# Two f tiles of the first side: down products as a 2x2 block product of 256-wide matmuls in place of 512-wide ones, its weights kept for the second side

## The chip, the cores and the metric

One core of a Trainium2 chip runs the whole program. The metric is the device time of one launch in microseconds (us). All figures below come from the page, the times and the trace of the kernel before.

## The reference, cut to what matters

The block is adaLN, a linear attention, a second adaLN and a gated bilinear MLP, all in float32, on one sequence of 2048 tokens with D = 512 and F = 1376. Only its last part is touched:

```
h = _layernorm(x) * (1 + cb) + sb          # x: 2048 x 512, after the attention
g = h @ w_gate                             # 512 x 1376
u = h @ w_up                               # 512 x 1376
x = x + gb * ((g * u) @ w_down)            # 1376 x 512
```

`gb` is a row of 512 factors; the kernel multiplies it into the rows of `w_down`.

## The kernel before

Every float32 operand of a matmul is split into a high part, rounded to the type that TensorE takes (`split`, L206 and L207: ScalarE writes the high part, VectorE or GpSimd the low part as a difference), and a product is three matmuls: high by high, high by low, low by high.

**The MLP.** The tokens are four chunks of 512; a side is two chunks: the first side is chunks 0 and 1, the second chunks 2 and 3. The hidden columns are 11 f tiles of 128 (the last, f 10, has 96). For each side and f tile one call of `block` makes gate and up for both chunks at once, as a 2x2 block product with 7 products instead of 8. Its left factors (`a11`, `s1`, `s2`, `a12`, `s3`, `a22`, `s4`) are pieces, sums and differences of the layer-normed tokens, its right factors the like of the weights. One product is 6 matmuls of 128x512 (L1057), so a block is 42, in the order a11, s1, s2, a12, s3, a22, s4. They go to four PSUM banks, which no other product uses.

Blocks are numbered 0 to 21 here, in their order on TensorE (`order` in the code). The first side's are 0 to 10 with f = 2, 3, 4, 5, 6, 7, 8, 9, 0, 1, 10; the second side's 11 to 21 with f = 0 to 10. Blocks 8 and 9 are thus f 0 and 1, and block 10 is f 10, of the first side; 11 and 12 are f 0 and 1 of the second.

**Down products.** The results of a block, `phi`, are the left operand of the down product, in which f is summed over. There are two ways:

- `down` (L1146 to L1148): for a group of f tiles, a chunk and some of its four quarters of 128 tokens, 3 matmuls of 128x512 for each f tile and quarter into a PSUM bank (`acc`, one of four), then a VectorE add into `x` (L1153) and, when it is the last, a DMA that writes the output. The first side's groups are f 2-3, 4-5, 6-7, 8-9 and 0-1-10. A group's four pieces (`fillers`) are spread over the blocks of the next group, in their point `pe`, between the fifth and the sixth product.
- `Pair` and `pair_steps` (L1223, L1250): two f tiles and two chunks form a 2x2 block product again, 7 steps for each two quarters; a step is 6 matmuls of 128x256, then VectorE adds of 128x256 into `x`. All pairs of f tiles of the second side go this way. `weight_sums` scales the two tiles of `w_down` (VectorE, L1277) and makes sums of them (GpSimd, L1204); `weight_splits` splits them (ScalarE L1214, GpSimd L1215). Steps stand in `queue`, from which each block takes up to 7, at its `POINTS`.

**What sets the order.** There is no scheduler: each engine runs its instructions in the order in which the code records them. A block has named points (`a11`, `s1`, `s2`, `a12`, `s3`, `pe`, `mid`, `s4`) to which jobs are hung (`at`). Nearly all DMAs are issued by SyncE (SP), in order, each after the instruction that it waits for and after the landing of the DMA eight places before it. Tiles come from one pool of 99 buffers, so that a DMA or an instruction may also wait for an older reader of its buffer.

**Transfers around the change.** The left factors of the second side are made during blocks 3 to 9 and written to DRAM (`aside`, L969); `fetch` (L983) brings back 28 tiles of 256 KB for block 11. Right factors are kept in DRAM too (L1034) and come back as 7 tiles for each block from 13 on (L1044); those of blocks 11 and 12 are still in their buffers. `load_down` (L111) loads a tile of `w_down`.

Of the kernel before, what the change touches and what calls it, by code (L numbers as in the profile page):

```python
# [11 lines left out]
ALU = mybir.AluOpType  # L12
# [10 lines left out]
def tile_adaln_block(  # L23
# [12 lines left out]
    nc = tc.nc  # L36
# [11 lines left out]
    NF = len(fts)  # L48
# [16 lines left out]
    def f32(ap):  # L65
        return ap.bitcast(F32)
# [339 lines left out]
    sums = {}  # L406
# [239 lines left out]
    for i in range(4, NT):  # L646
        ch, j = divmod(i, NJ)
        more = ch + 1 < NCH
# [129 lines left out]
    fs, tt = [], []  # L778
# [55 lines left out]
    pairs = [(cut(norm[2].t[k], 3 * P, 4 * P), wq[k]) for k in range(KD)]  # L834
# [230 lines left out]
    todo = []  # L1065
# [94 lines left out]
    class Pair:  # L1160
# [50 lines left out]
        def weight_splits(self, *ms):  # L1211
            for m in ms:
                h, l = B("w", dt=F32R), B("w", dt=F32R)
                nc.scalar.activation(h, self.raw[m], AF.Copy)  # L1214
                nc.gpsimd.tensor_tensor(l, self.raw[m], f32(h), op=ALU.subtract)  # L1215
# [56 lines left out]
    def load_down(f):  # L1272
        f0, n = fts[f]
        return load(w_down[f0:f0 + n, :], "raw")
# [4 lines left out]
    sides = [(0, 1), (2, 3)]  # L1279
# [102 lines left out]
    def split_down(s, f, low=None):  # L1382
        split_d[s, f] = split_raw(raw_d.pop((s, f)), low=low)
# [47 lines left out]
    pair_of = {f: g for g, fs in enumerate(groups) for f in fs[:2]}  # L1431
    weights = {}

    for n, (s, g, f) in enumerate(order):
        groups = groups_of[s]
        first, final = f == groups[g][0], f == groups[g][-1]
        if first:
            if before is not None and before[0] == 0:
                down_jobs(*before)
            for x in groups[g] if s == 0 else ():  # L1440
                raw_d[s, x] = load_down(x)
# [27 lines left out]
        if s == 0:  # L1469
# [3 lines left out]
        if n and order[n - 1][0] == 0:  # L1473
            at["s2"].insert(0, lambda s=order[n - 1][0], f=order[n - 1][2]: split_down(s, f))
# [9 lines left out]
        if s == 1 and f in pair_of:  # L1484
            at_first = f == groups[g][0]
            if at_first:
                pairs[g] = Pair()
                at["pe"].append(lambda xs=groups[g]: raw_d.update({(1, x): load_down(x) for x in xs}))
                sums = lambda g=g, x=groups[g]: pairs[g].weight_sums(raw_d[1, x[0]], raw_d[1, x[1]])
                if g:  # L1490
                    at["mid"].insert(0, sums)
            else:
                if not g:
                    at["s2"].append(sums)
                at["s3"] += [lambda g=g: pairs[g].weight_splits(0, 2)]
                at["mid"] += [lambda g=g: pairs[g].weight_splits(1, 3)]

            def done(i, t, p=pairs[g], at_first=at_first):
                p.f[(("a11", "a21") if at_first else ("a12", "a22"))[i]] = t
                if i == 0:  # L1500
                    todo.append(p.first if at_first else p.second)
        if s == 1:
            if n > NF + 1 and f in pair_of and first:
                queue += [x for js in ((0, 1), (2, 3)) for x in pair_steps(1, pairs[g - 1], js)]
            if f == tail:
                queue += pair_steps(1, pairs[g], (0, 1))
            if first and g:
                at["s2"].append(lambda p=pairs[g - 1]: (p.lows("s1", "s2"), p.second("s4")))
                at.setdefault("a12", []).append(lambda p=pairs[g - 1]: p.lows("a12", "s4", "a22"))
            elif f == tail:  # L1510
                at["s2"].append(lambda p=pairs[g]: (p.lows("s1", "s2"), p.second("s4")))
            for p in POINTS[4:] if n == NF + 2 else POINTS:
                at.setdefault(p, []).append(lambda: queue and queue.pop(0)())
            if f == tail:
                at["a12"].append(lambda p=pairs[g]: p.lows("a12", "s4", "a22"))
                at["s3"].append(lambda: split_down(1, tail))
# [27 lines left out]
    more = pair_steps(1, pairs[len(groups_of[1]) - 1], (2, 3), of=bank, also=with_tail)  # L1544
# [38 lines left out]
```

## Time and profile before

| what | us |
|---|---|
| median of 3 runs (554.57 to 554.84) | 554.71 |
| the profiled execution | 554.69 |
| its span, first to last instruction | 552.5 |
| TensorE busy in it, 2739 matmuls | 546.7 |
| VectorE / ScalarE / GpSimd busy | 421.0 / 297.4 / 177.4 |
| L1057, 924 matmuls of the blocks, busy union | 220.2 |
| L1146 to L1148, 276 matmuls of `down`, busy union | 107.6 |
| L1223, 420 matmuls of the pairs, busy union | 91.8 |

The span is the reading of the trace; 2.2 us of the execution lie around it. Matmuls are pipelined and their ends are modelled, so the duration of one (390 ns at 128x512, 282 ns at 128x256) is longer than the time from its start to the next one's start, which is what it costs. Block times are read from one first matmul to the next: on TensorE blocks 8, 9, 10, 11, 12, 13 and 14 start at 330.62, 345.58, 357.82, 370.29, 388.08, 405.86 and 417.56 us, and block 15 at 432.20.

### The profile page before, as it was taken

How to read it: one execution, taken by the hardware profiler on the slowest of the kernel's cores; microseconds unless marked ns; L12 is line 12 of the kernel's file. 1: busy time of each engine (PE TensorE's matmuls, PEld its weight loads, DVE VectorE, ACT ScalarE, POOL GpSimd, SP SyncE). 2: the span in 40 equal slices, each digit the busy share in tenths (PEclk: the TensorE clock that was granted, in tenths of full speed). 3: DMA queues.
4: the chain of work that ended last, by engine and by line, in shares of the span. 5: the costliest groups of instructions: out<-in, count | busy, mean ns of one | idle time of the engine just before them, and what ended most of it. 6: DMA issues, size and time to landing. Idle time of an engine off the chain costs nothing.

```text
span 552.5 us, 8033 instructions
## 1 busy us (share of the span) xinstructions
PE 546.7 (99%) x2739; PEld 459.7 (83%) x2739; DVE 421.0 (76%) x764; ACT 297.4 (54%) x532; POOL 177.4 (32%) x183
## 2 busy tenths in 40 slices
PE   8999999999999999999999999999999999999997
PEld 6888888888888888888888888878888888888886
DVE  6978779978998998865656767854567877879696
ACT  4875858456467876654545355432442534453540
POOL 2000000003537645353556644400512524242400
PEclk9999999999999999999999999999999999999999
DMA  8910224203230045195888635499585534342004
GB/s 258 374 55 1 76 77 152 77 0 78 78 114 2 0 161 182 39 319 177 285 286 273 223 123 206 152 377 324 176 261 200 180 124 141 129 144 87 0 1 152
DMA packets 58800, 83.75 MB, mean 152 GB/s; under 512 B 6596, under 2 KB 23752, under 8 KB 58760
## 3 DMA queue, kind: packets, MB, share of 16 engines
q1 hardware_dynamic: 56832, 81.68, 43.6%
q10 hardware_dynamic: 1928, 1.58, 0.9%
q8 instruction: 21, 0.34, 0.3%
q14 instruction: 19, 0.16, 0.1%
HBM read 53.54 MB, written 29.69 MB: 151 GB/s over the span
## 4 chain that ended last, share of the span: by engine, by line
PE 99%; DVE 0%; issue 0%
PE bank L1057 38%; PE acc L1223 8%; PE acc L871 8%; PE bank L219 5%; PE bank L221 5%; PE bank L220 5%; PE acc L1146 4%; PE acc L1147 4%; PE acc L1148 4%; PE acc L372 3%; PE acc L374 3%; PE acc L373 3%; PE bank L284 2%; PE acc L459 2%; PE acc L153 1%; PE bank L846 1%
## 5 line engine op out<-in xcount | busy, mean ns | idle before, releaser
L1057 PE MATMUL bank<-h,w 128*128 128x512 f32 (+1 forms) x924 | 220.2, 391 | 0.0
L1057 PEld LDWEIGHTS bank<-h,w 128*128 128x128 f32 (+1 forms) x924 | 168.8, 186 | 36.2
L1063 ACT ACTIVATE bank<-bank 128x512 f32<-128x512 f32 (+2 forms) x46 | 26.2, 571 | 131.0 <-PE bank L1057 130.8
L1020 POOL TENSOR_TENSOR w<-raw,w 128x256 fp32r<-128x256 f32 (+3 forms) x22 | 24.2, 1099 | 78.8 <-ACT w L1013 64.0
L1250 DVE TENSOR_TENSOR x<-acc,x 128x256 f32<-128x256 f32 x108 | 39.2, 414 | 10.6 <-PE acc L1223 9.9
L1223 PE MATMUL acc<-w,kh 128*128 128x256 f32 x252 | 46.8, 282 | 0.0
L219 PE MATMUL bank<-w,h 128*128 128x512 f32 x112 | 44.1, 394 | 0.0
L1223 PEld LDWEIGHTS acc<-w,kh 128*128 128x128 f32 x252 | 41.4, 191 | 2.9
L221 PE MATMUL bank<-w,h 128*128 128x512 f32 x112 | 43.7, 390 | 0.0
L220 PE MATMUL bank<-w,h 128*128 128x512 f32 x112 | 43.7, 390 | 0.0
L871 PE MATMUL acc<-w,xh 128*128 128x512 f32 x128 | 40.7, 399 | 0.0
L1083 DVE TENSOR_TENSOR phi<-bank,g 128x512 f32<-128x512 f32 (+1 forms) x22 | 15.1, 688 | 29.9 <-PE bank L1057 28.4
L712 POOL TENSOR_TENSOR f<-h,zb 128x512 f32<-128x512 f32 x12 | 17.5, 1470 | 63.0 <-ACT zb L692 48.9
L262 POOL TENSOR_TENSOR rstd<-ve,half 128x4 f32<-128x4 f32 (+3 forms) x12 | 10.6, 885 | 82.2 <-DVE ve L259 68.1
L1113 DVE TENSOR_TENSOR g<-bank,u 128x512 f32<-128x512 f32 (+1 forms) x22 | 15.2, 690 | 28.4 <-ACT u L1063 27.0
L1146 PE MATMUL acc<-w,kh 128*128 128x512 f32 (+1 forms) x92 | 35.9, 390 | 0.0
L1147 PE MATMUL acc<-w,kh 128*128 128x512 f32 (+1 forms) x92 | 35.9, 390 | 0.0
L1148 PE MATMUL acc<-w,kl 128*128 128x512 f32 (+1 forms) x92 | 35.8, 389 | 0.0
L1223 PE MATMUL acc<-w,kl 128*128 128x256 f32 x126 | 35.6, 283 | 0.0
L1063 ACT ACTIVATE u<-bank 128x512 f32<-128x512 f32 (+1 forms) x44 | 26.1, 594 | 12.6 <-PE bank L1057 12.4
L1153 DVE TENSOR_TENSOR x<-acc,x 128x512 f32<-128x512 f32 x44 | 28.0, 680 | 5.9 <-PE acc L1148 5.8
L1020 POOL TENSOR_TENSOR w<-t,w 128x512 fp32r<-128x512 f32 (+1 forms) x22 | 29.6, 1344 | 0.0
(202 smaller groups left out, 1184.0 us busy)
## 6 DMA issues: line engine op xcount, KB each, us to landing
right<-w SPq DMA_DIRECT2D x56, 256.0 KB, 3.6
w<-right SPq DMA_DIRECT2D x56, 256.0 KB, 3.7
x<-in_A_x_dram SPq DMA_DIRECT2D x22, 256.0 KB, 5.2
raw<-in_w_mod_dram SPq DMA_DIRECT2D x22, 256.0 KB, 3.7
raw<-in_B_w_down_dram SPq DMA_DIRECT2D x20, 256.0 KB, 3.0
side_s<-h SPq DMA_DIRECT2D x16, 256.0 KB, 2.8
h<-side_s SPq DMA_DIRECT2D x16, 256.0 KB, 6.0
raw<-in_A_wqkv_dram SPq DMA_DIRECT2D x12, 256.0 KB, 6.0
```

The costliest lines, as they stand in the source:

```text
L219: nc.tensor.matmul(ps, ah, bh, start=begin and i == 0, stop=False)
L220: nc.tensor.matmul(ps, ah, bl, start=False, stop=False)
L221: nc.tensor.matmul(ps, al, bh, start=False, stop=end and i == n - 1)
L871: nc.tensor.matmul(yps[i], x, y, start=fresh and k + n == 0, stop=k == KD - 1 and n == 2, skip_group_check=True)
L1020: sub = lambda out, x, y: (on or nc.gpsimd).tensor_tensor(out, x, f32(y), op=ALU.subtract)
L1057: mm = lambda x, y, **kw: nc.tensor.matmul(ps, x[:, k], y, skip_group_check=True, **kw)
L1063: nc.scalar.activation(out, x, AF.Copy)
L1146: nc.tensor.matmul(dn[j], hh[:n, a:b], dh[:n], start=i == 0, stop=False)
L1147: nc.tensor.matmul(dn[j], hh[:n, a:b], dl[:n], start=False, stop=False)
L1148: nc.tensor.matmul(dn[j], hl[:n, a:b], dh[:n], start=False, stop=i == n_of - 1)
L1223: mm = lambda x, y, **kw: nc.tensor.matmul(ps, x[:, a:b], y, skip_group_check=True, **kw)
L1250: nc.vector.tensor_tensor(xt[:, halves[at]], banks[b][m], xt[:, halves[at]], op=ALU.add)
```

## The change

1. The first side's group 0-1-10 is taken apart. f 0 and 1 become a `Pair` on chunks 0 and 1: 14 steps in `queue`, taken 3 in block 10, 7 in block 11 and 4 in block 12. f 10 alone goes by `down` in 8 pieces of 3 matmuls (`alone`), one quarter each, at the points s3, pe, mid and s4 of blocks 11 and 12, each with its add and its output DMA.
2. The second side's first pair, also f 0 and 1, takes over the split weights of that pair (`p.d = pairs[same[s, g]].d`); its own loads, scalings, sums and splits go. The first pair's sums are made in block 9 (GpSimd), its splits there too, with the low parts on VectorE instead of GpSimd.
3. The four pieces of group 8-9 are placed two in block 8 and two in block 9 (before two, one and one, in blocks 8, 9 and 10).
4. The tiles of `w_down` for f 0 and 1 are loaded in block 8 at point `pe`, that of f 10 in block 10.
5. `fetch` moves: before from block 9's point pe on, in the order a11, a12, s1, s2, s3, a22, s4; now in block 10, a11, s1, s2, a12, s3, and last a22 and s4, one name a point.

```diff
-        def first(self):
+        def early(self):
             self.sum("s3", nc.vector)
             self.split("a11", nc.vector)
+
+        def first(self):
+            self.early()
             self.split("s3", nc.vector)
...
-    pair_of = {f: g for g, fs in enumerate(groups) for f in fs[:2]}
-    weights = {}
+    paired = {(0, g) for g in [4]} | {(1, g) for g in range(len(groups))}
+    pair_of = {(s, f): (s, g) for s, g in paired for f in groups_of[s][g][:2]}
+    same = {(1, 0): (0, 4)}
+    points = POINTS
+    alone = [lambda j=j, c=c: down(sides[0][c], [hs[0, tail][c]], [split_d[0, tail]], (j,), True)()
+             for js in ((0, 1), (2, 3)) for c in range(2) for j in js]
...
-        after = len(groups[g]) - groups[g].index(f)
+        after = max(len(groups[g]) - groups[g].index(f) - (s == 0 and f in groups_of[0][4] and (0, 4) in paired), 1)
...
-        if s == 0 and n == 9:
-            after_side = {}
-            at["pe"].append(lambda: fetch(stash, after_side, "a11", "a12"))
         edge = s == 0 and n + 1 < len(order) and order[n + 1][0] == 1
         if edge:
-            at["a11"].append(lambda: fetch(stash, after_side, "s1", "s2"))
-            at["s1"].insert(0, lambda: fetch(stash, after_side, "s3"))
-            at["s2"].insert(0, lambda: fetch(stash, after_side, "a22", "s4"))
+            after_side = {}
+            for x, names in (("s1", ("a11",)), ("s2", ("s1",)), ("a12", ("s2",)), ("s3", ("a12",)), ("pe", ("s3",)), ("s4", ("a22", "s4"))):
+                at.setdefault(x, []).insert(0, lambda names=names: fetch(stash, after_side, *names))
...
+                if (s, g) in same:
+                    p.d = pairs[same[s, g]].d
...
+                for x, ms in ((("s3", (0, 2)), ("mid", (1, 3))) if s else ((("a12", (0, 1)), ("s3", (2, 3))))):
+                    at.setdefault(x, []).insert(0, lambda s=s, p=p, ms=ms: p.weight_splits(*ms, on=None if s else nc.vector))
...
+        if was and was[:2] in paired and was[2] == groups_of[was[0]][was[1]][1]:
+            of, p = was[0], pairs[was[:2]]
+            points = POINTS if queue else POINTS[4:]
+            queue += [x for js in ((0, 1), (2, 3))[:1 if (s, f) == (1, tail) else 2] for x in pair_steps(of, p, js)]
...
+            else:
+                at["s2"].append(lambda p=p: p.second("s1", "s2"))
+                at.setdefault("a12", []).append(lambda p=p: p.lows("s1", "s2", "a22", "a12"))
+                at["pe"].append(lambda p=p: p.second("s4"))
+                at["s4"].append(lambda p=p: p.lows("s4"))
...
+        if s == 1 and alone:
+            for x in ("s3", "pe", "mid", "s4"):
+                at[x].insert(0, lambda: alone.pop(0)())
```

How it moves instructions, at three places. Lines from `first` on stand three lower in the changed kernel: the pair matmuls are L1226 there, the pair adds L1253, the scaling of `w_down` L1280; L1146 to L1153 keep their numbers.

TensorE in block 10, from the end of its fifth product (`bank`) on. The rows are the last matmul of that product, the six of the pair's first step and the first one of its second step; before, 12 matmuls of `down` (group 8-9) stood here.

```order
L1057 MATMUL bank_2389<-h_2383,w_4037 96x512
L1226 MATMUL acc_4196<-w_3982,kh_3949 128x256
L1226 MATMUL acc_4196<-w_3983,kh_3949 128x256
L1226 MATMUL acc_4196<-w_3982,kl_3950 128x256
L1226 MATMUL acc_4196<-w_3982,kh_3949 128x256
L1226 MATMUL acc_4196<-w_3983,kh_3949 128x256
L1226 MATMUL acc_4196<-w_3982,kl_3950 128x256
L1226 MATMUL acc_4205<-w_4000,kh_4135 128x256
```

A step of the pair (six rows for two quarters of 128 tokens) takes the place of a piece of `down`, and the next step follows at once.

VectorE at the end of block 12, before. `x` are the token tiles that the down products are added to (L1153; the last is x_133); phi, g and phi are the end of the block.

```order
L1113 TENSOR_TENSOR g_4404<-bank_2390,u_4402 128x512
L1153 TENSOR_TENSOR x_127<-acc_4414,x_127 128x512
L1153 TENSOR_TENSOR x_129<-acc_4415,x_129 128x512
L1153 TENSOR_TENSOR x_131<-acc_4434,x_131 128x512
L1153 TENSOR_TENSOR x_133<-acc_4435,x_133 128x512
L1083 TENSOR_TENSOR phi_4483<-bank_2389,g_4404 128x512
L1122 TENSOR_TENSOR g_4482<-bank_2390,u_4392 128x512
L1083 TENSOR_TENSOR phi_4486<-g_4394,g_4482 128x512
```

The same place in the changed kernel:

```order
L1113 TENSOR_TENSOR g_4518<-bank_2390,u_4516 128x512
L1153 TENSOR_TENSOR x_99<-acc_4520,x_99 128x512
L1153 TENSOR_TENSOR x_101<-acc_4526,x_101 128x512
L1153 TENSOR_TENSOR x_131<-acc_4538,x_131 128x512
L1083 TENSOR_TENSOR phi_4551<-bank_2389,g_4518 128x512
L1122 TENSOR_TENSOR g_4550<-bank_2390,u_4490 128x512
L1083 TENSOR_TENSOR phi_4554<-g_4492,g_4550 128x512
L1153 TENSOR_TENSOR x_133<-acc_4556,x_133 128x512
```

The last add, x_133, has moved behind the three instructions that end the block; its matmuls are now the last three of block 12 on TensorE.

SP behind that add, in the changed kernel. It is the output DMA of that tile, then the seven right factors of block 14, then the two tiles of `w_down` of the second side's second pair.

```order
L1155 DMA out_dram<-x_131 128x512
L1155 DMA out_dram<-x_133 128x512
L1044 DMA w_4562<-right_0_2558 128x512
L1044 DMA w_4564<-right_1_2560 128x512
L1044 DMA w_4566<-right_2_2562 128x512
L1044 DMA w_4568<-right_3_2564 128x512
L1044 DMA w_4570<-right_4_2566 128x512
L1044 DMA w_4572<-right_5_2568 128x512
L1044 DMA w_4574<-right_6_2570 128x512
L111 DMA raw_4642<-in_B_w_down_dram 128x512
L111 DMA raw_4644<-in_B_w_down_dram 128x512
```

On SP the order of this piece is as before, with the same 11 DMAs; only the add that its second row waits for has moved.

More of the change, by code (lines that the diff above doesn't have):

```diff
@@ L1214, in weight_splits @@
                 nc.scalar.activation(h, self.raw[m], AF.Copy)
-                nc.gpsimd.tensor_tensor(l, self.raw[m], f32(h), op=ALU.subtract)
+                (on or nc.gpsimd).tensor_tensor(l, self.raw[m], f32(h), op=ALU.subtract)
                 for i, n in enumerate((("b11", None), ("b21", "b22"), ("t1", "t2"), ("t3", "t4"))[m]):
@@ L1472, in tile_adaln_block @@
             at["s2"] += [lambda: scale_down(raw_d[1, tail])]
-        if n and order[n - 1][0] == 0:
-            at["s2"].insert(0, lambda s=order[n - 1][0], f=order[n - 1][2]: split_down(s, f))
-        if s == 0 and n == 9:
-            after_side = {}
-            at["pe"].append(lambda: fetch(stash, after_side, "a11", "a12"))
+        was = order[n - 1] if n else None
+        if was and was[0] == 0 and (0, was[2]) not in pair_of:
+            at["s2"].insert(0, lambda f=was[2]: split_down(0, f))
@@ L1499, in done @@
                 p.f[(("a11", "a21") if at_first else ("a12", "a22"))[i]] = t
                 if i == 0:
[L1501 to L1516, printed above, removed]
+                    todo.append((p.first if at_first else p.second) if s else p.early if at_first else lambda: p.second("a22", "a12"))
@@ L1517, in tile_adaln_block @@
+        for x in points if queue else ():
+            at.setdefault(x, []).append(lambda: queue and queue.pop(0)())
+        points = POINTS
+        if s == 1 and alone:
+            for x in ("s3", "pe", "mid", "s4"):
+                at[x].insert(0, lambda: alone.pop(0)())
+        if f == tail and s == 1:
+            at["s3"].append(lambda: split_down(1, tail))
         hs[s, f] = block(side, rights.pop(n), at=at, done=done, s4_first=(s, f) == (1, tail), d_first=n == 1)
@@ L1542, in tail_half @@
             two[m].dma_start(ov[ch, j][:, part], xt[:, part])
-    more = pair_steps(1, pairs[len(groups_of[1]) - 1], (2, 3), of=bank, also=with_tail)
+    more = pair_steps(1, pairs[1, len(groups_of[1]) - 1], (2, 3), of=bank, also=with_tail)
     rest = lambda c, *js: down(sides[1][c], [hs[1, tail][c]], [split_d[1, tail]], js, True)()
```

41 lines of the change are left out of this document (24 added, 17 removed).

## The prediction

> **What bounds the kernel now.** I read the page first: the busy times, then the chain that ended last.
>
> ```profile
> PE 546.7 (99%) x2739; PEld 459.7 (83%) x2739; DVE 421.0 (76%) x764; ACT 297.4 (54%) x532; POOL 177.4 (32%) x183
> PE 99%; DVE 0%; issue 0%
> ```
>
> TensorE is busy for 546.7 of 552.5 us and is 99% of the chain, so the time is a sum of matmuls plus what TensorE waits. "Busy" is no price, though, since matmuls overlap. The price is the distance of starts, read from the timeline of TensorE, here around a piece of `down` in block 7:
>
> ```profile
> 315.20 7.42 PE L1057 MATMUL bank<-h,w 128*128 128x512 f32 x32
> 322.46 0.39 PE L1146 MATMUL acc<-w,kh 128*128 128x512 f32 x1
> ...
> 327.90 3.33 PE L1057 MATMUL bank<-h,w 128*128 128x512 f32 x14
> ```
>
> 32 matmuls last 7.42 us, of which the last one's 0.39: 31 distances of 0.227. The 24 of `down` take 327.90 - 322.46 = 5.44, also 0.227 each. Now two steps of a pair, in block 13, and block 14's beginning:
>
> ```profile
> 403.12 9.71 PE L1057 MATMUL bank<-h,w 128*128 128x512 f32 x42
> 412.66 0.40 PE L1223 MATMUL acc<-w,kh 128*128 128x256 f32 x2
> ...
> 414.10 2.91 PE L1057 MATMUL bank<-h,w 128*128 128x512 f32 x12
> ...
> 417.56 2.91 PE L1057 MATMUL bank<-h,w 128*128 128x512 f32 x12
> ```
>
> Twelve 256-wide matmuls take 414.10 - 412.66 = 1.44, so 0.120 each: a little over half. I then took whole blocks, a `down` block (66 matmuls of 512) and a pair block (42 of 512, 42 of 256):
>
> ```profile
> 315.66:330.62 14.96, 14.96 (x68) 12.39 (x66) 9.97 (x16) 8.25 (x16) 7.76 (x8) 1.00 0.39 127
> 432.20:446.84 14.64, 14.64 (x87) 12.91 (x86) 12.93 (x26) 6.04 (x11) 5.61 (x6) 1.00 0.48 163
> ```
>
> Both are full (busy equals length; the counts take in neighbours that reach in) at a granted clock of 1.00. The reader is to see 14.96 against 14.64: 42 narrow matmuls in place of 24 wide ones save 0.32 us.
>
> **TensorE's part of the change.** f 0 and 1 on two chunks cost 2 x 2 x 4 x 3 = 48 wide matmuls by `down`, and 14 steps x 6 = 84 narrow ones by the pair. That is twice the exchange just read: **-0.64 us**. By single distances it is 84 x 0.120 - 48 x 0.227 = -0.82; the whole blocks also hold the slightly longer distances after a change of width, so I take -0.64. f 10's 24 matmuls stay, as does the number of blocks; moving pieces of group 8-9 from block 10 to 9 costs nothing in sum. From block 13 on, every block has as many steps as before (3, then 7), because the queue is empty at the end of block 12.
>
> The Trainium skill prices it otherwise: "TensorE: Matmul & The Clock Gate", section "Back-to-back issue gap", gives an isolated gap of N/2.4 + 2.5 ns, an estimated 216 and 109 ns here, so -1.2 us. The rows' 227 and 120 ns do not bear it out.
>
> **Block 9, new weight work.** Two scalings, four GpSimd sums, four splits are squeezed ahead of f 10's own splits, which block 10 needs.
>
> ```profile
> 347.49 2.47 DVE L1153 TENSOR_TENSOR x<-acc,x 128x512 f32<-128x512 f32 x4
> ...
> 354.80 0.37 ACT L1013 ACTIVATE w<-raw 128x192 fp32r<-128x192 f32 x1
> 355.25 1.01 POOL L1020 TENSOR_TENSOR w<-raw,w 128x192 fp32r<-128x192 f32 x1 [7.23 <-DVE h L207]
> ...
> 392.89 1.06 POOL L1204 TENSOR_TENSOR t<-raw 128x256 f32<-128x256 f32 x1 [33.71 <-DVE raw L1277]
> 394.61 1.55 POOL L1204 TENSOR_TENSOR t<-raw,t 128x256 f32<-128x256 f32 x2
> ```
>
> The adds end at 349.9; VectorE then has four instructions and a scaling at 0.6 each (347.49's four take 2.47), to 353.0; the sums take 392.89 to 396.16, 3.3 us, to 356.3; ScalarE's last two pair splits and two others follow, so that f 10's first high part comes at about 357.9 instead of 354.80, and GpSimd's first low part ends at 359.3. With 66 matmuls block 9 now ends at 345.58 + 14.96 = 360.5, and the third matmul of block 10, which needs it, starts at 361.0. Cover left: 1.7 us. The next low part comes at 360.3 and is wanted at 362.4. Cost 0; a delay over 1.7 us would be paid in full. The four low parts moved from GpSimd to VectorE have room: VectorE's list for that block is 18 instructions of some 0.65, 12 of 15 us.
>
> **The fetch.** Before:
>
> ```profile
> 356.64 3.91 SPq L983 DMA_DIRECT2D h<-side_a  x8
> 360.64 9.31 SPq L983 DMA_DIRECT2D h<-side_s  x12
> ...
> 373.01 2.32 SPq L983 DMA_DIRECT2D h<-side_s  x4
> ```
>
> ```profile
> DMA to landing us min/median/max: 3.1/5.3/7.5
> ```
>
> 28 tiles go out over 18.7 us (356.64 to 375.33), and land 5.3 later. In the new order the first is issued near 360.4 (behind the last stash of s4, whose low part VectorE ends near 359). Even with the same pace and latency all have landed by 384.4. Block 11 starts near 372.3 (block 10 is 42 x 0.23 + 18 x 0.12 = 11.8 long), wants a11 at once (four tiles, landed by about 366) and s4 only at its last product, near 386.9; a22, near 384.9, goes out before s4. Buffer waits hold a22 and s4 until block 10's sixth product, 369.8, which leaves 15 us for eight tiles. Cost 0, cover 2.5 us for s4 at the old pace.
>
> **Block 13's loads, where I see the price.** SP waits in order. Before, the fourth add of block 12 came early:
>
> ```profile
> 395.71 0.69 DVE L1113 TENSOR_TENSOR g<-bank,u 128x512 f32<-128x512 f32 x1 [2.36 <-ACT u L1063]
> ...
> 402.62 1.38 DVE L1153 TENSOR_TENSOR x<-acc,x 128x512 f32<-128x512 f32 x2 [2.75 <-PE acc L1148]
> ...
> 406.06 0.69 DVE L1122 TENSOR_TENSOR g<-bank,u 128x512 f32<-128x512 f32 x1 [0.67 <-PE bank L1057]
> 406.79 0.69 DVE L1083 TENSOR_TENSOR phi<-g,g 128x512 f32<-128x512 f32 x1
> ...
> 415.15 1.28 DVE L1277 TENSOR_TENSOR raw<-raw,row 128x512 f32<-128x512 f32 x2
> 416.36 0.68 DVE L1083 TENSOR_TENSOR phi<-bank,g 128x512 f32<-128x512 f32 x1
> 417.04 0.69 DVE L1122 TENSOR_TENSOR g<-bank,u 128x512 f32<-128x512 f32 x1
> ```
>
> and SP could go on:
>
> ```profile
> 399.21 5.16 SPq L1155 DMA_DIRECT2D out_dram<-x  x4
> 404.46 3.27 SPq L1044 DMA_DIRECT2D w<-right  x7
> 407.87 0.99 SPq L111 DMA_DIRECT2D raw<-in_B_w_down_dram  x2
> ```
>
> ```profile
> L111 SPq DMA_DIRECT2D raw<-in_B_w_down_dram x2: 337/475/613, 407.9 to 408.2; - x2
> DMA to landing us min/median/max: 6.5/6.7/6.8
> ```
>
> Call the end of block 12 E (before: 403.12 + 12 x 0.227 = 405.85). The seven loads started at E - 1.4, and the second `w_down` tile landed at 408.2 + 6.8 = 415.0, just before the scaling took it. Now that add is last in the block. Its matmuls follow the last product, so L1122 starts 3 x 0.227 = 0.68 earlier than E + 0.2 (406.06 shows the 0.2), at E - 0.5; phi follows 0.73 later, the add 0.6 after that, and ends at E + 1.55. SP's loads start 0.45 behind it, at **E + 2.0, 3.4 us later** than before. The load of the first tile that block 14 needs has 9 us left; but the two `w_down` tiles have little. Their scalings stand in VectorE's queue ahead of phi and g (415.15, 416.36, 417.04), and block 14's second product overwrites the bank that g reads. From the second scaling's start (415.8) to g's end (417.73) are 2.0 us. The product is due at 417.56 + 6 x 0.227 = 418.9, which is E + 13.06.
>
> How long do the nine loads take? Before, 415.0 - 404.46 = 10.6 us, so g would end at E + 2.0 + 10.6 + 2.0 = E + 14.6 and TensorE wait 1.6 us. The DMA rate shows that this is not the queue at its best:
>
> ```profile
> 404.00:406.50 2.50, 2.50 (x12) 2.06 (x12) 1.14 (x3) 0.00 (x0) 0.00 (x0) 1.00 0.94 274
> 406.50:409.00 2.50, 2.50 (x12) 2.07 (x12) 2.24 (x4) 1.52 (x3) 0.32 (x1) 1.00 0.92 269
> 409.00:411.50 2.50, 2.50 (x12) 2.06 (x12) 1.76 (x3) 1.72 (x4) 0.97 (x1) 1.00 1.02 305
> 411.50:414.00 2.50, 2.50 (x18) 2.27 (x17) 1.63 (x4) 2.24 (x5) 0.00 (x0) 1.00 1.06 403
> ```
>
> The last column is GB/s: some 280 for 7.5 us, then 403. At 403 throughout, a tile of 256 KB takes 0.65 us; with the first landed after 3.1 (the least in the fetch's row) and eight more behind it, the burst takes 8.3: g at E + 12.3, no wait. So the bounds are **0 and 1.6 us**. The row of this very burst is the nearest, but two output writes stood just ahead of it (404.0 and 403.4), and now one does, the other some 2.5 us earlier; I take 10.2 us, a wait of **1.2 us**. The phi and g that wait hold up nothing else: the steps of block 14 keep their distance to it, and GpSimd's sums, 3 us later, are not wanted before the splits in block 14's fifth product.
>
> **Accumulators.** Eight single pieces now claim `acc` banks, of which a set of steps holds three. The tightest claim is in block 11: after the fifth product come two pieces and a step, 0.68 + 0.68 + 0.73 = 2.1 us, then a step that needs the first piece's bank. VectorE's g there ends 1.5 us after that product (395.71 + 0.69, the product having ended at 388.08 + 30 x 0.227 = 394.9), and the add behind it at 2.1. The others have 0.4 or more by the same count. Cost 0 to 0.5, taken as 0. VectorE's further adds and splits lie beside matmuls and hold up nobody by the same count.
>
> **Sum.** Against the profiled execution, 554.69 (0.02 under the median): -0.64 + 1.2 = +0.56, so **555.2 us**.
>
> **Rivals.** (a) *The loads are hidden*: the burst takes under 9 us, and only the matmuls count: 554.69 - 0.64 = 554.05. For it speaks the 403 GB/s, against it the 280 just after output writes. (b) *Accumulator turnover, slower*: each add waits behind others on VectorE, and the claims of single pieces and steps in blocks 11 and 12 find their bank still read. It decides once VectorE is one add (0.6 us) behind; five claims then wait 0.3 to 0.6 each, 1.5 to 3 us, on top of the 0.56: 556.7 to 558, I say 557. Against it: VectorE stood idle 2.36 us before the row 395.71. (c) *The exchange is worth more*: the wide ones that go were dear (block 10: 12.47 us over 54, 0.231 each), the narrow ones come at 0.120, so 84 x 0.120 - 48 x 0.231 = -1.0, and no wait: 553.7. Against it: 0.231 is seen in that block alone. The formula of the Trainium skill named above would give 553.5. (d) *It does not do what it says*, the counts of matmuls being other than 48 and 84: the order of both kernels shows 36 more rows on TensorE, so hardly; 554.7.
>
> **Chances.** Forecast 0.55, (a) 0.22, (b) 0.16, (c) 0.05, (d) 0.02. The measurement can tell about 0.2%, that is 1.1 us, from no change. Below 553.6 lies much of (c) and the lucky end of (a): faster 0.04. Beyond 555.8 lie (b) and the end of the forecast where the burst takes 10.8 us or more (0.07): slower 0.23. The rest, 0.73, is within. For 8 in 10 the range leaves out most of (b) and (c): 553.9 to 556.4; cases within 0.2% of no change hold most of the chance.
>
> **What would show it.** Right: blocks 15 to 20 still 14.64 apart; blocks 8 to 13 some 0.6 to 0.9 us shorter in sum; the seven loads after the last output DMA of the first side at 2.0 behind block 12's end; TensorE idle or late by about 1 us before the second product of block 14, VectorE's scaling waiting for a DMA of `w_down`. Wrong: gaps in blocks 10 to 12 behind L1153 or L1253 (b), behind L983 (the fetch), or behind L1020 at block 10's beginning (weight work); or no gap at all in block 14 (a).

## The result and the profile after

The changed kernel takes **555.66 us** (median of 16 runs, 555.05 to 556.60) against 554.63 (16 runs, 554.51 to 555.11): 1.03 us more, ratio 1.0019 with an interval of 1.0011 to 1.0027. The forecast was 555.2, its range 553.9 to 556.4. The profiled execution of the changed kernel took 555.82 (span 553.4), that of the kernel before 554.69 (552.5).

The page of the changed kernel, busy times and the engines of the chain:

```profile
PE 546.1 (99%) x2775; PEld 460.0 (83%) x2775; DVE 432.5 (78%) x794; ACT 299.7 (54%) x535; POOL 177.6 (32%) x180
PE 94%; DVE 3%; DMA 2%; issue 0%; ACT 0%; POOL 0%; DVEq 0%; ACTq 0%; POOLq 0%
```

TensorE has 36 more matmuls and is busy 0.6 us less, as the exchange should make it. But the chain, 99% TensorE before, now leaves it for 5% of the span: something else is waited for. These 5% are no price: the chain counts all the work that leads to a wait, some 8 us in block 14 for a loss of 0.53. TensorE's waits in the changed kernel (the kernel before has the first row only):

```profile
PE acc L153 <- DVE w L148: 2.0, 1, 2.0
PE bank L295 <- ACT n L277: 1.0, 1, 1.0
PE acc L1226 <- DVE x L1253: 0.4, 1, 0.4
PE bank L1057 <- DVE g L1122: 0.2, 1, 0.2
```

L295 is at the kernel's start, which the change does not touch; the other two are its own. A wait row counts only the idle part. What a wait costs is read better from the distances of blocks, each from its first matmul (L1057) to that of the next; "all" runs from block 0 to the end of the last matmul. All lengths are in us, each from one profiled execution:

| kernel | block 0 starts | 9 | 10 | 11 | 12 | 13 | 14 | 21 | all |
|---|---|---|---|---|---|---|---|---|---|
| before | 205.94 | 12.24 | 12.47 | 17.79 | 17.79 | 11.69 | 14.64 | 28.63 | 342.73 |
| changed | 206.28 | 14.96 | 11.99 | 17.58 | 15.26 | 11.70 | 15.17 | 29.27 | 343.41 |
| e1 lows last | 205.91 | 14.96 | 12.41 | 17.57 | 15.26 | 11.70 | 16.06 | 28.62 | 344.06 |
| e2 store behind loads | 205.85 | 14.96 | 11.87 | 17.59 | 15.26 | 11.70 | 14.64 | 29.28 | 342.78 |
| e3 both | 206.94 | 14.96 | 11.87 | 17.59 | 15.26 | 11.70 | 14.64 | 28.62 | 342.12 |
| e10 both again | 206.15 | 14.96 | 11.87 | 17.57 | 15.26 | 11.70 | 14.64 | 28.62 | 342.10 |
| e4 before, lows first | 206.48 | 12.24 | 12.45 | 17.79 | 17.79 | 11.69 | 14.64 | 29.25 | 343.32 |

Blocks 0 to 8 take 139.64 and blocks 15 to 20 87.84 in all of them. The table says where the time went: blocks 9 to 13 are 0.49 shorter (71.49 against 71.98), block 14 is 0.53 longer and block 21 is 0.64 longer, together +0.68. Block 0 also starts 0.34 later; that start moves between 205.85 and 206.94 in executions whose code up to there is the same, so it is not counted here. Whether the change moves it is left open below.

**Block 14** is the wait that was forecast. SyncE's queue of the changed kernel around block 12's end (E, 405.72), and the chain of waits in block 14:

```profile
407.27 0.33 SPq L1155 DMA_DIRECT2D out_dram<-x  x1
407.69 3.25 SPq L1044 DMA_DIRECT2D w<-right  x7
411.06 1.05 SPq L111 DMA_DIRECT2D raw<-in_B_w_down_dram  x2
```

```profile
411.06 5.55 DMA raw<-in_B_w_down_dram
...
416.63 0.59 DVE raw L1280
...
417.24 0.68 DVE raw L1280
417.92 0.60 DVE phi L1083
418.52 0.61 DVE g L1122
...
419.18 0.98 PE bank L1057 x3
```

The loads start at E + 1.97 (before: E - 1.4). The first scaling starts at its tile's landing (416.61), the second right behind it at 417.24 (its tile had landed at 417.17), and phi, g and the second product follow in a line: every link is one that the prediction named.

**Block 21** was not forecast. VectorE there, before and after:

```profile
528.77 1.40 DVE L1250 TENSOR_TENSOR x<-acc,x 128x256 f32<-128x256 f32 x4
530.09 0.68 DVE L1172 TENSOR_TENSOR kl<-phi,kh 128x512 fp32r<-128x512 f32 x1
530.69 0.68 DVE L1172 TENSOR_TENSOR kl<-s,kh 128x512 fp32r<-128x512 f32 x1
```

```profile
529.15 0.68 DVE L1172 TENSOR_TENSOR kl<-phi,kh 128x512 fp32r<-128x512 f32 x1
530.06 0.69 DVE L1172 TENSOR_TENSOR kl<-s,kh 128x512 fp32r<-128x512 f32 x1 [0.23 <-ACT kh L1168]
530.67 1.41 DVE L1253 TENSOR_TENSOR x<-acc,x 128x256 f32<-128x256 f32 x4
```

The order is turned round. Before, the code had a line of its own for the last block, which put the low parts behind the steps of point `a12`; the changed code treats all blocks with a pair alike and puts them ahead. The adds that free the accumulators thus come 1.5 us later against their block, and a following step waits.

### The profile page after: what moved, and what is told of

Same layout as the page of the kernel before. It is cut to its first block, busy times and chain, and to the rows that moved or that the text cites. A ratio compares the mean times of both kernels' runs of the same rounds, so it can differ in the third digit from the quotient of the medians.

```text
span 553.4 us, 8143 instructions
## 1 busy us (share of the span) xinstructions
PE 546.1 (99%) x2775; PEld 460.0 (83%) x2775; DVE 432.5 (78%) x794; ACT 299.7 (54%) x535; POOL 177.6 (32%) x180
## 4 chain that ended last, share of the span: by engine, by line
PE 94%; DVE 3%; DMA 2%; issue 0%; ACT 0%; POOL 0%; DVEq 0%; ACTq 0%; POOLq 0%
PE bank L1057 36%; PE acc L1226 9%; PE acc L871 8%; PE bank L219 5%; PE bank L221 5%; PE bank L220 5%; PE acc L1147 3%; PE acc L1146 3%; PE acc L1148 3%; PE acc L372 3%; PE acc L374 3%; PE acc L373 3%; PE bank L284 2%; PE acc L459 2%; PE bank L846 1%; DMA raw<-in_B_w_down_dram 1%
## 5 line engine op out<-in xcount | busy, mean ns | idle before, releaser
L1057 PE MATMUL bank<-h,w 128*128 128x512 f32 (+1 forms) x924 | 222.2, 391 | 0.2 <-DVE g L1122 0.2
L1057 PEld LDWEIGHTS bank<-h,w 128*128 128x128 f32 (+1 forms) x924 | 168.1, 186 | 36.4 <-DVE g L1122 0.6
L1063 ACT ACTIVATE bank<-bank 128x512 f32<-128x512 f32 (+2 forms) x46 | 26.2, 571 | 123.8 <-PE bank L1057 123.6
L1253 DVE TENSOR_TENSOR x<-acc,x 128x256 f32<-128x256 f32 x132 | 48.0, 415 | 12.9 <-PE acc L1226 12.2
L1226 PE MATMUL acc<-w,kh 128*128 128x256 f32 x308 | 57.4, 283 | 0.4 <-DVE x L1253 0.4
L1226 PEld LDWEIGHTS acc<-w,kh 128*128 128x128 f32 x308 | 50.6, 191 | 4.4 <-DVE x L1253 0.6
L1020 POOL TENSOR_TENSOR w<-raw,w 128x256 fp32r<-128x256 f32 (+3 forms) x22 | 24.7, 1124 | 73.7 <-ACT w L1013 64.1
L1226 PE MATMUL acc<-w,kl 128*128 128x256 f32 x154 | 43.5, 283 | 0.0
L1063 ACT ACTIVATE u<-bank 128x512 f32<-128x512 f32 (+1 forms) x44 | 26.2, 595 | 15.4 <-PE bank L1057 15.2
L1083 DVE TENSOR_TENSOR phi<-bank,g 128x512 f32<-128x512 f32 (+1 forms) x22 | 15.1, 687 | 24.2 <-PE bank L1057 24.2
L1113 DVE TENSOR_TENSOR g<-bank,u 128x512 f32<-128x512 f32 (+1 forms) x22 | 15.2, 690 | 21.2 <-ACT u L1063 19.9
L1020 POOL TENSOR_TENSOR w<-t,w 128x512 fp32r<-128x512 f32 (+1 forms) x22 | 29.7, 1351 | 0.0
L1153 DVE TENSOR_TENSOR x<-acc,x 128x512 f32<-128x512 f32 x44 | 27.8, 680 | 2.3 <-PE acc L1148 2.3
L1147 PE MATMUL acc<-w,kh 128*128 128x512 f32 (+1 forms) x76 | 29.6, 390 | 0.0
L1146 PE MATMUL acc<-w,kh 128*128 128x512 f32 (+1 forms) x76 | 29.6, 390 | 0.0
L1148 PE MATMUL acc<-w,kl 128*128 128x512 f32 (+1 forms) x76 | 29.6, 389 | 0.0
```

The lines of the kernel that those rows point to most:

```text
L1020: sub = lambda out, x, y: (on or nc.gpsimd).tensor_tensor(out, x, f32(y), op=ALU.subtract)
L1057: mm = lambda x, y, **kw: nc.tensor.matmul(ps, x[:, k], y, skip_group_check=True, **kw)
L1063: nc.scalar.activation(out, x, AF.Copy)
L1146: nc.tensor.matmul(dn[j], hh[:n, a:b], dh[:n], start=i == 0, stop=False)
L1147: nc.tensor.matmul(dn[j], hh[:n, a:b], dl[:n], start=False, stop=False)
L1148: nc.tensor.matmul(dn[j], hl[:n, a:b], dh[:n], start=False, stop=i == n_of - 1)
```

## The experiments

Each was timed beside the kernel before on the same chip; B is the median of the kernel before there, which moves from 554.77 to 555.13 between chips. All but e4 start from the changed kernel.

**e1, the order of the last block alone is taken back.**

```
-                at.setdefault("a12", []).append(lambda p=p: p.lows("a12", "s4", "a22"))
+                if f != tail:
+                    at.setdefault("a12", []).append(lambda p=p: p.lows("a12", "s4", "a22"))
...
+        if s == 1 and f == tail:
+            at["a12"].append(lambda p=p: p.lows("a12", "s4", "a22"))
```

> The changed kernel, with one side effect taken back: in the last block, VectorE's three low parts (L1172) again stand behind the two steps' adds, as before the change. Theory A (the low parts ahead of the adds hold an accumulator that the following step of the last block claims, the wait of 0.64 us at 531.47): the wait goes, 555.66 - 0.64 = 555.0. Rival B (the wait there is VectorE being busier in general, and the order is not its cause): 555.66, with the same gap in the last block.

Measured: 555.95, B 554.83. Block 21 is back at 28.62, as A says. The median did not fall; the 12 runs spread from 554.38 to 559.92. In the traced execution block 14 lost 1.42 us instead of 0.53 and block 10 took 0.42 more than in the changed kernel; the other runs are not traced. The chain in block 14 shows the landing: the same load from the same place, 0.83 us slower.

```profile
411.09 6.38 DMA raw<-in_B_w_down_dram
...
417.50 0.71 DVE raw L1280 x2
```

So the price of block 14's wait was set by the landing in these two executions, 0.53 and 1.42; block 10 is told below.

**e2, the last store of the first side behind block 14's loads.**

```
-    alone = [lambda j=j, c=c: down(sides[0][c], [hs[0, tail][c]], [split_d[0, tail]], (j,), True)()
+    alone = [lambda j=j, c=c: down(sides[0][c], [hs[0, tail][c]], [split_d[0, tail]], (j,), (c, j) != (1, 3))()
...
+        if n == NF + 2:
+            at["pe"].append(lambda: nc.sync.dma_start(ov[1, 3], xts[1][3]))
```

> The changed kernel, with the last store of the first side's output put behind block 14's seven right factors and the two w_down loads in SP's queue; its add stays where it is. Theory A (SP stands at that store until the add is done, so the loads start late and the scaling on VectorE holds block 14's second product): the loads start 3 us earlier, the 0.5 us gap of block 14 goes, 555.66 - 0.5 = 555.15, and the runs, which spread over 1.55 us, spread over some 0.6 as before the change, since the landing of a load no longer sets the end. Rival B (the burst is slow whenever it starts, or another transfer decides): the gap and the spread stay, 555.66.

Measured: 555.40, B 554.83. SyncE's queue and VectorE's scaling:

```profile
404.46 3.26 SPq L1044 DMA_DIRECT2D w<-right  x7
407.81 1.08 SPq L111 DMA_DIRECT2D raw<-in_B_w_down_dram  x2
```

```profile
414.47 1.28 DVE L1280 TENSOR_TENSOR raw<-raw,row 128x512 f32<-128x512 f32 x2
```

The loads start 2.7 us earlier against block 12's end (E - 0.71, with E at 405.17 there), the scaling waits for nothing and block 14 is 14.64: A on the mechanism. A's spread is wrong: the runs still spread from 554.48 to 556.40, so the landing was not the only thing that varied.

**e3, both edits.**

> The changed kernel with both edits (low parts behind the adds in the last block, the last store behind the loads). Theory A (the two waits hide a gain of the exchange of matmuls, which the blocks 9 to 13 show as 0.49 us): 555.66 - 0.64 - 0.5 = 554.5, or counted from the kernel before 554.63 - 0.49 = 554.15; so 554.15 to 554.5, slightly faster than before. Rival B (the exchange gains nothing by itself, what the blocks show is a shift in time that is lost elsewhere): 554.6 to 555.0, not faster than before.

Measured: 554.85, B 554.83, ratio 0.9996 (0.9984 to 1.0008). The trace gives A: no wait in blocks 10, 14 and 21, 342.12 against 342.73. The median gives B's "not faster". e10 repeats it.

**e4, the kernel before with nothing but the turned order of the last block.**

```
+            if f == tail:
+                at.setdefault("a12", []).append(lambda p=pairs[g]: p.lows("a12", "s4", "a22"))
             for p in POINTS[4:] if n == NF + 2 else POINTS:
...
-                at["a12"].append(lambda p=pairs[g]: p.lows("a12", "s4", "a22"))
```

> The kernel before, with nothing of the change but the order of the last block: VectorE's three low parts ahead of the two steps' adds. Theory A (this order costs the wait by itself): 554.63 + 0.64 = 555.27, with a gap of some 0.6 us in the last block. Rival B (the wait of the changed kernel comes from elsewhere): 554.63.

Measured: 555.66, B 554.83, ratio 1.0026 (1.0013 to 1.0040). Block 21 is 29.25, +0.62, and TensorE's waits now have the changed kernel's row:

```profile
PE acc L1223 <- DVE x L1250: 0.4, 1, 0.4
```

With e1 this is shown from both sides: the turned order costs 0.6 us by itself.

**Block 10.** In e1 the third matmul of block 10, which needs f 10's first low part (L1020), and the one behind it lose 0.42 us together against e3:

```profile
361.31 3.02 PE L1057 MATMUL bank<-h,w 128*96 128x512 f32 x12 [0.17 <-POOL w L1020]
```

The chain leads from there over that low part back to GpSimd's sums of block 9 (L1207). GpSimd in e1 and in e3:

```profile
353.08 2.93 POOL L1207 TENSOR_TENSOR t<-raw 128x256 f32<-128x256 f32 x1 [5.02 <-DVE raw L1280]
355.97 0.72 POOL L1207 TENSOR_TENSOR t<-raw,raw 128x256 f32<-128x256 f32 x1
356.66 1.55 POOL L1207 TENSOR_TENSOR t<-raw,t 128x256 f32<-128x256 f32 x2
360.25 1.01 POOL L1020 TENSOR_TENSOR w<-raw,w 128x192 fp32r<-128x192 f32 x1 [2.04 <-DVE h L207]
```

```profile
354.11 1.12 POOL L1207 TENSOR_TENSOR t<-raw 128x256 f32<-128x256 f32 x1 [5.03 <-DVE raw L1280]
355.19 1.18 POOL L1207 TENSOR_TENSOR t<-raw,raw 128x256 f32<-128x256 f32 x1
356.33 2.33 POOL L1207 TENSOR_TENSOR t<-raw,t 128x256 f32<-128x256 f32 x2
```

The first sum took 1.06 in block 12 before; here it takes 2.93 in one execution and 1.12 in another, 7.53 us behind the block's start in both.

In the changed kernel it took 2.92, but began 7.10 behind the block's start, because VectorE's phi (L1083) some 6 us before it took 0.69 there and 1.12 in e1. So f 10's first low part was ready at 361.21, and the third matmul started at 361.35 without a wait. The 0.12 by which block 10 is longer there than in e3 lies at its sixth product, which starts at 369.30, right behind ScalarE's copy to u (L1063, done at 369.25); e1 has it too, so that its 0.54 over e3 is 0.42 and 0.12.

VectorE beside the sums, in the changed kernel (GpSimd's first sum took 2.92, from 353.02) and in e3:

```profile
353.46 0.68 DVE L1172 TENSOR_TENSOR kl<-s,kh 128x512 fp32r<-128x512 f32 x1
354.06 1.28 DVE L1218 TENSOR_TENSOR w<-raw,w 128x512 fp32r<-128x512 f32 x2
355.27 0.68 DVE L1113 TENSOR_TENSOR g<-bank,u 128x512 f32<-128x512 f32 x1
```

```profile
354.55 1.22 DVE L1172 TENSOR_TENSOR kl<-s,kh 128x512 fp32r<-128x512 f32 x1
355.70 2.37 DVE L1218 TENSOR_TENSOR w<-raw,w 128x512 fp32r<-128x512 f32 x2
```

Either GpSimd stands while VectorE runs three subtractions at full pace, or VectorE's take twice as long while GpSimd's go through. Only the first makes f 10's parts late enough to be waited for. The code up to there is the same in the changed kernel, e1, e2, e3 and e10; the sum stands in the first two and goes through in the other three. The Trainium skill states such a thing on the page "SBUF — State Buffer", section "Who interferes with whom": a VectorE instruction with two inputs in SBUF contends with a GpSimd instruction that reads SBUF, and the order of issue decides which one blocks. The rows agree with the first part: GpSimd's sum of 353.02 gets through beside L1113, which reads a bank and one SBUF tile. They do not bear out the second: in both kernels the sum started during VectorE's second scaling (L1280), and yet it stood through three more instructions in one and went through in the other. The other experiments try to use this.

**e5, the four sums on VectorE** (on top of e3).

```
-            sub = lambda out, x, y: nc.gpsimd.tensor_tensor(out, x, y, op=ALU.subtract)
+            sub = lambda out, x, y: (on or nc.gpsimd).tensor_tensor(out, x, y, op=ALU.subtract)
...
-                    sums = lambda s=s, p=p, x=groups[g]: p.weight_sums(raw_d[s, x[0]], raw_d[s, x[1]])
+                    sums = lambda s=s, p=p, x=groups[g]: p.weight_sums(raw_d[s, x[0]], raw_d[s, x[1]], None if s else nc.vector)
```

> The kernel with both edits, and the four sums of the new weight work in block 9 (L1207) on VectorE instead of GpSimd. Theory A (the third matmul of block 10 waits in some runs, 0.34 us in the one trace, because GpSimd's sums stand up to 1.9 us while VectorE's subtractions run beside them, so that f 10's low parts come late; on VectorE they take some 1.5 us in its own queue, which has room): block 10 is 11.87 in every trace, the spread of the runs falls to that of the kernel before, and the median is 0.6 us under the kernel before of the same chip. Rival B (what spreads the runs of the version with both edits lies elsewhere, such as at the start of the kernel): as that version, equal to the kernel before within 0.2 us.

Measured: 555.41, B 555.13; block 10 is 13.26, 1.39 longer. A failed. GpSimd now starts f 10's low parts early, and these stand against VectorE's two splits of left factors, which took 1.29 in the changed kernel:

```profile
359.34 2.92 DVE L207 TENSOR_TENSOR h<-s,h 128x512 fp32r<-128x512 f32 x2
362.18 0.68 DVE L1083 TENSOR_TENSOR phi<-bank,g 128x512 f32<-128x512 f32 x1
362.78 0.67 DVE L1122 TENSOR_TENSOR g<-bank,u 128x512 f32<-128x512 f32 x1
```

Block 9's g ends at 363.45, and block 10's second product, which overwrites the bank it reads, starts at 363.60. (The view of waits names ScalarE's split of phi, L1168, which ended at 363.56. That is not what is needed: in the changed kernel this product starts at 362.27, before that split's 362.96.)

**e6, e5 with the fetch of the left factors at its old points.**

> The same kernel as the one with the sums on VectorE, but the second side's left factors are fetched at the old points (from block 9's fifth product on) instead of the new ones. Theory A (the later fetch is covered and neither costs nor gains): within 0.1 us of that kernel. Rival B (the early fetch holds SP at buffers that are not free yet, or fills the queues before f 10's loads): slower by 0.5 us or more, with a gap in blocks 10 to 12.

Measured: 574.81, B 555.13. Rival B, by far more than it said: block 10 takes 32.60. The chain there:

```profile
365.41 5.29 DMA h<-side_a
...
370.72 5.97 DMA h<-side_s
...
376.75 5.36 DMA h<-side_a
...
382.13 5.18 DMA right<-w
...
387.41 0.60 ACT u L1063
```

The fetch stands one load behind the other, the stores of f 10's weights behind them, and ScalarE's copy behind those. So the later fetch is no independent part of the change: with the new work of blocks 9 and 10 as it stands, the old fetch points cost 19 us. What each load waits for was not traced further.

**e7, e5 with weights of its own for the second side's first pair** (`same = {}`).

> The same kernel as the one with the sums on VectorE, but the second side's first pair loads, sums and splits weights of its own instead of sharing the first side's. Theory A (the sharing takes work off VectorE, GpSimd and the loads, none of which TensorE waits for there): within 0.1 us of that kernel. Rival B (the extra weight work of blocks 11 and 12, beside the adds of the first side, makes the steps late): slower by 0.5 us or more, with gaps in blocks 12 and 13.

Measured: 558.62, B 555.13. Rival B: against e5, block 12 is 1.95 longer (17.21) and block 13 0.34 (12.04). The sharing carries 2.3 us in these blocks, which I had counted as work off the path. The medians differ by 3.2 us; in the traces another 1.14 lie behind the last matmul (5.14 us to the span's end, 4.00 in e5), for a reason that is not shown.

**e8, e3 with the four low parts of block 9 (L1218) on GpSimd.**

> The kernel with both edits, but the four low parts of the new weight work in block 9 (L1218) on GpSimd, as the other pairs have them, and the sums there too. Theory A (there is no cover left between GpSimd's work of block 9 and block 10's third matmul: four low parts of 1.3 us, from 357.0 to 362.2, and f 10's first one of 1.0 us behind them, 363.2, against 362.0 where it is due): a wait of 1.2 us in block 10 in every run, so 1.2 us above the version with the sums on VectorE. Rival B (the prediction's cover of 1.7 us holds with the low parts on VectorE; 5.2 us more on GpSimd then cost 3.5): 3.5 us above it.

Measured: 557.18, B 555.13; block 10 is 14.50. That is 1.24 over e5, as A says, but e5 waits there itself; over e3, which does not wait, it is 2.63, between the two numbers. GpSimd, and VectorE's two splits in the same stretch:

```profile
357.65 2.56 POOL L1218 TENSOR_TENSOR w<-raw,w 128x512 fp32r<-128x512 f32 x2
360.16 3.42 POOL L1218 TENSOR_TENSOR w<-t,w 128x512 fp32r<-128x512 f32 x2
```

```profile
358.92 3.54 DVE L207 TENSOR_TENSOR h<-s,h 128x512 fp32r<-128x512 f32 x2 [2.56 <-ACT h L206]
```

No cover is left, as A says, and the two engines stretch each other once more (3.42 for 2.56, 3.54 for 1.29).

**e9, e5 with block 9's last two splits behind its phi and g.**

```
-            at["s3"].append(lambda: some(2))
+            at["s3"].append(lambda: some(0 if n == 9 else 2))
-            at["s4"].append(lambda: some(2 if n > 4 else 0))
+            at["s4"].append(lambda: some(4 if n == 9 else 2 if n > 4 else 0))
```

> The kernel with both edits and the sums on VectorE, and in block 9 the two last splits of the second side's left factors (L206, L207) behind the block's own phi and g instead of ahead of them. Theory A (VectorE and GpSimd hold each other up when both read two operands of SBUF at once: there the two L207, 0.6 us each alone, took 2.92 us beside GpSimd's low parts, so that g came late for block 10's second product by 1.36 us): phi and g, which read a bank, come first, block 10 is 11.87 us, no gap of over 0.1 us remains but the one of block 11, and from block 0's start to the end it is 0.6 us less than the kernel before (342.1 against 342.73); the median is 0.4 to 0.6 us under the kernel before of the same chip, as much as the spread of its start lets be seen. Rival B (the later splits make the fetch of the left factors late, as the block with the old fetch points waited 16 us, or the adds behind them hold accumulators): gaps in blocks 10 and 11, slower than the kernel before.

Measured: 558.55, B 554.77. The gap at block 10's second product is gone, but rival B costs more: block 10 is 13.12, waiting at its sixth product for ScalarE's copy to u, and block 11 20.83 instead of 17.59, since the left factors, stored and fetched later, are waited for.

```profile
PE bank L1057 <- ACT u L1063: 0.8, 1, 0.8
PE bank L1057 <- DMA h<-side_a: 0.7, 3, 0.3
PE bank L1057 <- DMA h<-side_s: 0.2, 1, 0.2
```

**e10, e3 once more, on another chip.**

> The version with both edits (low parts behind the adds in the last block, the last store behind the loads) once more, beside the one before. Theory A: GpSimd's sums in block 9 go through or stand, from execution to execution, so block 10 is 11.87 in some and 12.2 to 12.5 us in others, and the median lies 0 to 0.4 us under the kernel before. Rival B (the kernel gains nothing): at or over the kernel before.

Measured: 554.76, B 554.77, ratio 1.0001 (0.9992 to 1.0009), runs from 553.92 to 556.11 where B's go from 554.57 to 555.23. The trace has 342.10 and again no wait in blocks 10, 14 and 21. At equal medians with a wider spread in both directions, some executions are faster and some slower than before; that block 10's wait makes the slow ones fits e1, but no trace of this kernel shows it.

**e11, e3 with f 10's weights ahead of the pair's in block 9** (`right_split` at `s1` instead of `s3`).

> The version with both edits, and in block 9 f 10's high and low parts (L1013, L1016, L1020) ahead of the new weight work of the pair instead of behind it, so that GpSimd makes them from about 3 us after the block's start, and the four sums follow. Theory A (what still spreads the runs is block 10's wait for f 10's low parts, behind sums of GpSimd that stand beside VectorE's work; the pair's own weights are not wanted before block 10's fifth product, 7 us later): block 10 is 11.87 us, the stretch from block 0 to the end 342.1, the runs spread over 0.7 us like those of the kernel before, and the median is 0.5 to 0.6 us under the kernel before of the same chip. Rival B (the spread comes from elsewhere, or f 10's early parts wait for buffers of weights and hold ScalarE's copies): equal to the kernel before or slower, with a gap in block 9.

Measured: 555.57, B 554.97. Rival B, though not for buffers: GpSimd's parts now meet other VectorE work, in its row for two splits that took 1.28 in the other kernels,

```profile
350.51 2.69 DVE L207 TENSOR_TENSOR h<-f,h 128x512 fp32r<-128x512 f32 x2
```

and all that follows on VectorE is later: block 9 takes 15.43, block 10 12.84 (behind g).

**e12, e3 with the splits of the two sums in block 10.**

```
-                for x, ms in ((("s3", (0, 2)), ("mid", (1, 3))) if s else ((("a12", (0, 1)), ("s3", (2, 3))))):
+                for x, ms in ((("s3", (0, 2)), ("mid", (1, 3))) if s else (("a12", (0, 1)),)):
...
+        if n == NF - 1:
+            at["s1"].append(lambda p=pairs[0, 4]: p.weight_splits(2, 3, on=nc.vector))
```

> The version with both edits, and the splits of the two sums (L1217 and L1218 of t, two high and two low parts) in block 10 instead of block 9; the sums stay on GpSimd. Theory A (block 9 has too much for VectorE and GpSimd together, since they hold each other up; 1.3 to 1.5 us of VectorE's work moved to block 10, where its first user is the second step at 7.6 us, brings f 10's parts and block 9's phi and g 1.2 us or more forward in every execution): block 10 is 11.87 us, the stretch from block 0 to the end 342.1, the runs spread less than the 554.2 to 555.4 of the version with both edits, and the median is 0.3 to 0.6 us under the kernel before of the same chip. Rival B (block 10 has no room either: the low parts of the pair's s1 and s2, 1.3 us later on VectorE, make the steps wait): a gap in block 10's second half, equal to the kernel before or slower.

Measured: 555.49, B 554.99. Rival B: f 10's parts come early, but block 10 is 12.68, waiting 0.6 for ScalarE's copy to u (L1063), which stands behind ScalarE's splits of the pair's s1 and s2; VectorE made those sums only after the two low parts that were moved there. Block 10 has no room either. No version is faster than the kernel before; e3 is the best, equal to it.

## Why the prediction was right, and where it was not

- **The exchange, -0.64.** Right. Where block 10 does not wait (e3, e10), blocks 9 to 13 take 71.38 and 71.36 against 71.98: -0.61, with 0.17 lost in it at the one accumulator of block 11 that the prediction put at 0 to 0.5 (two distances of 0.19 and 0.22 us where 0.12 is usual; VectorE's add L1153 ends just before). Without that loss it is -0.78, nearer to the -0.82 by single distances than to the -0.64 that was taken, so that -0.64 met the measured -0.61 in part by luck.
- **Block 14's loads, 1.2 of 0 to 1.6.** Right in every link and in its bounds, too large for the changed kernel's trace: loads at E + 1.97 (said: 2.0), the wait 0.53 there and 1.42 in e1's. The burst, 10.2 in the prediction, took 9.5 (407.69 to 417.17) and 10.4 (407.73 to 418.15). Undone in e2, the wait goes.
- **Block 9, cost 0 with 1.7 us of cover.** Wrong in the cover. The step that failed is "the sums take 392.89 to 396.16, 3.3 us": a duration read in block 12, where VectorE stood idle from 393.35 on. Beside VectorE's new low parts the sums took 5.1 (353.02 to 358.15). Of the cover 0.14 was left in the changed kernel's trace, where f 10's low part cost nothing, and in e1's it cost 0.42. The 0.12 that block 10 loses in both lies behind ScalarE's copy, for which the prediction has no term.
- **"VectorE's further adds and splits lie beside matmuls and hold up nobody".** Wrong in the last block, 0.64, which is more than the forecast wait cost in the same trace. I had read the order around the change and took blocks 15 to 21 to be as before because their counts of matmuls were. One line that treated the last block differently was gone in the diff.
- **The fetch, cost 0.** Right as a cost; that it carries 19 us (e6) was not seen.
- **The sum.** The forecast was +0.56, the median +1.03; one trace's sum is -0.61 + 0.12 + 0.53 + 0.64 = +0.68, so that blocks 9 to 13 are 0.49 shorter and not the 0.6 to 0.9 that were to show it right. That the total came near is luck: the 0.64 of block 21 was missing, and block 14's wait was 0.67 smaller than priced. The other 0.35 of the 1.03 between the medians is not shown. Rival (b) was right that accumulators would be late, but in blocks 11 and 12 only one was, by 0.17; the one that cost 0.64 is in block 21.
- **Open.** Without the two waits e3 is 0.6 us shorter from block 0 to the end in both its traces (e3, e10), and still equal in its medians. In these two traces block 10 does not wait, and yet their spans are 553.1 and 552.4 against 552.5. What makes up for the gain in them lies outside the blocks: block 0 starts 1.00 and 0.21 later than in the trace before, and from the last matmul to the span's end it takes 4.00 and 4.18 us against 3.86. Whether that is chance is not shown. For chance speaks that block 0 starts at 206.31 on average in the 12 traces with the change, and at 205.94 and 206.48 in the two without; against it, that the 16 runs of the kernel before differ by 0.60 in all, while these starts differ by 1.09. How often block 10 waits in the runs without a trace stays open too.

## What to carry to other kernels

Removing matmuls pays by the distance of starts, here 0.6 us, and only as long as the work that feeds the new form fits: look at the block that prepares the operands, and take the durations of VectorE and GpSimd for it from rows in which both are at work, not from a block where one of them mostly stands idle (the sums: 3.3 us there, 5.1 here). When code for several cases is merged, compare the order of instructions in the first and the last block too, not only where the change is. A store that waits for the last add holds every load behind it in its queue; put it behind the loads that are wanted first.

## What the runs showed of the hardware

- A GpSimd subtraction of 128x256 took 1.06 us in block 12 before, with VectorE idle from 0.46 us after its start on, and 2.92 beside three VectorE subtractions in a row, all of which it waited out; two VectorE splits of 128x512 take 1.28, and 2.7 to 3.5 beside GpSimd's. Which engine stands can differ between executions with the same start to 0.01 us (e1, e3).
- The same nine loads of 256 KB from the same place took 9.5 and 10.4 us to their last landing in the changed kernel and e1, and 10.2 to 10.6 in e2, e3, e10 and the kernel before, where they started earlier.
